# Block-diagonal state of a retention kernel: four full-width products in place of eight half-width column-tiled ones

## The chip, the cores and the metric

The kernel runs on one core of one Trainium2 chip. The time is device time in microseconds (us), the median of several executions. Executions of one kernel mostly agree within 0.3%, so a change of 1% is visible and one of 0.2% is not. TensorE (PE) is the matmul engine; its weight loads are listed separately as PEld. DVE, ACT and POOL are the other engines.

Three words are used throughout. A *full-width* product has 128 rows and 128 columns of weights. A *column-tiled* (half-width) product has 128 rows and 64 columns of weights and writes only 64 output partitions; two of them, in different column halves of the array, can run at once. A *row-tiled* product has 64 rows of weights and runs two at a time in the same way. The *columns* of a product are those of its moving operand, which is streamed past the weights. These are three tiling modes of the array.

## The reference, cut to what matters

```python
scores = scale * q @ k^T                      # 8 batches, 8 heads, 576 positions, 64 per head
ret    = scores * where(i >= j, gamma_h ** (i - j), 0)
x      = heads side by side of (ret @ v)      # 4608 x 512
out    = ((x @ w_a) * (x @ w_b)) @ w_out      # 512 -> 1536 -> 512
```

## The kernel before

The sequence is cut into 36 chunks of 128 tokens, nine for every two batches. Within a chunk, masked scores times v give one part of the output. The earlier chunks enter through a running state, k^T v, a 64x64 block for each head. Two heads share one 128x128 tile of the state, which is therefore block-diagonal (the blocks off the diagonal are zeros). Both parts are accumulated in the same tile `o` of PSUM, the memory for matmul results:

```python
    def outputs(i, halves=False):
        ...
        o = ps_att.tile([128, HP, 128], FP32, tag="att", name="o")   # HP = 4 head pairs
        if m > 0:                                  # a chunk with a state before it
            st = state_of.pop(i)
            n = 64 if m == MID else 128            # the middle chunk of nine spans two batches
            for p in range(HP):
                for hi in (0, 1):                  # state product, column-tiled
                    nc.tensor.matmul(o[64 * hi:64 * hi + 64, p, 0:n],
                                     st[:, p, 64 * hi:64 * hi + 64],
                                     qkT[:, 0, p, 0:n],
                                     start=(p == 0), stop=True,
                                     skip_group_check=True)
        for p in range(HP):
            for hi in (0, 1):                      # masked product, column-tiled
                e0 = p * 128 + 64 * hi
                nc.tensor.matmul(o[64 * hi:64 * hi + 64, p, :],
                                 vb[:, e0:e0 + 64], sT[:, hi, p, :],
                                 start=(m == 0 and p == 0), stop=True,
                                 skip_group_check=True)
```

The rest of TensorE's work is the feed-forward part: full-width products, most of 512 moving columns. The attention of later chunks is put into that stream in three stages, mostly for two adjacent chunks at a time:

```python
    def second_stage(g):
        for i in g[1:]:
            state(i)              # k^T v ("kv"), full-width (64 rows in the middle chunk)
        for i in g:
            scores(i)             # row-tiled

    def third_stage(g):
        flush()
        for i in g:
            outputs(i)            # the code above, for both chunks in one run
```

Of the kernel before, what the change touches and what calls it, by code (L numbers as in the profile page):

```python
# [18 lines left out]
def kernel(  # L19
# [19 lines left out]
    nc = tc.nc  # L39
# [17 lines left out]
    def rows_of(i):  # L57

        b, m = 2 * (i // PER), i % PER
        if m < MID:  # L60
            return [(0, 128, b, 128 * m)]
        if m == MID:
            return [(0, 64, b, 128 * m), (64, 64, b + 1, 0)]
        return [(0, 128, b + 1, 64 + 128 * (m - MID - 1))]
# [201 lines left out]
    def outputs(i, halves=False):  # L266
        m = i % PER
        qkb, qb, kb, vb = natural.pop(i)
        qkT = transposed.pop(i)
        sT = scored.pop(i)  # L270
        o = ps_att.tile([128, HP, 128], FP32, tag="att", name="o")
        if m > 0:
            st = state_of.pop(i)
            n = 64 if m == MID else 128
            for p in range(HP):
                for hi in (0, 1):
                    nc.tensor.matmul(o[64 * hi:64 * hi + 64, p, 0:n],  # L277
                                     st[:, p, 64 * hi:64 * hi + 64],
                                     qkT[:, 0, p, 0:n],
                                     start=(p == 0), stop=True,  # L280
                                     skip_group_check=True)
        for p in range(HP):
            for hi in (0, 1):
                e0 = p * 128 + 64 * hi
# [4 lines that stand above are left out]
        s0 = rows_of(i)[0][3]  # L289

        def scaled(c0, c1):
            nc.vector.tensor_tensor(  # L292
                xT[:, c0:c1, i * 128:(i + 1) * 128], o[:, c0:c1],
                qs[:, c0:c1, s0:s0 + 128], op=ALU.mult)

        if halves:
            later.append(lambda: scaled(0, HP // 2))
            later.append(lambda: scaled(HP // 2, HP))
        else:
            later.append(lambda: scaled(0, HP))  # L300
# [83 lines left out]
    for i in range(4):  # L384
        if idle[i][0]:
            warm(idle[i][0])
        scores(i)
        flush()
        if i == 2:
            load_w(0, W1)  # L390
            load_w(W1, W2)
        if i < 3:
            cast(i + 1, "dve" if i == 2 else "act")
        state(i)
        if idle[i][1]:
            warm(idle[i][1])
        if i < 3:
            transposes(i + 1)
            outputs(i)
            flush()  # L400
    load_w(W2, DFF)
    for i in (0, 1, 2):
        load_wo(i)
    outputs(3, halves=True)
    flush()
    nc.sync.dma_start(gate, wo_sb[0:1, 3, 0:64])
# [39 lines left out]
# [3 lines that stand above are left out]
            outputs(i)  # L449
# [73 lines left out]
```

## Time and profile before

| | before |
|---|---|
| median of 3 executions | 346.77 us (345.89 to 347.11) |
| span of the profiled execution | 877.8 us |
| TensorE busy | 97% of the span |
| feed-forward products, in units of 512 columns | 1296 |
| half-width state products / masked products | 256 / 288 |

These are lines of the profile page of that execution: the span, the busy time of each engine (with its share of the span and the number of instructions), and the chain of waits that ended last, by engine.

```profile
span 877.8 us, 6134 instructions
...
PE 854.0 (97%) x2390; PEld 309.4 (35%) x2426; DVE 162.0 (18%) x272; ACT 112.6 (13%) x229; POOL 84.3 (10%) x121
...
PE 97%; issue 2%; DMA 1%; SPq 0%; POOL 0%; DVE 0%; ACT 0%
```

TensorE holds 97% of that chain, so what changes its stream should change the time. But the span is two and a half times the timed one, and this page has no row for TensorE's granted clock. Its durations can't be taken as costs. The spacing between matmuls can still be read, because it falls into a few sharp values: most 512-column products start 621 ns apart, others 485, and 128-column ones 56 or about 189 ns. Each is 53 to 56 ns per 128 columns plus a whole number of stalls of about 136 ns.

The timeline of TensorE around the outputs of one pair of chunks shows what the change is about. Columns: start in us, length in us, engine, line of the kernel, operation, output <- inputs, weights as rows*columns, moving operand, number.

```profile
start us, us, engine line op out<-in xcount [idle before <-releaser]
305.81 0.79 PE L349 MATMUL po<-wo_sb,hT 128*128 128x512 bf16 x1
306.52 0.69 PE L277 MATMUL o<-qkT,state_166 128*64 128x128 bf16 x8
306.90 0.93 PE L285 MATMUL o<-sT,vb 128*64 128x128 bf16 x8
307.52 0.80 PE L277 MATMUL o<-qkT,state_167 128*64 128x128 bf16 x8
308.14 0.80 PE L285 MATMUL o<-sT,vb 128*64 128x128 bf16 x8
309.26 0.92 PE L349 MATMUL po<-wo_sb,hT 128*128 128x512 bf16 x1 [0.32 <-issue]
```

Eight half-width state products (L277) or masked products (L285) take 0.62 us from the start of one group to the start of the next (307.52 to 308.14), which is the same as one 512-column product takes in this execution. So the eight ran as four pairs of 128 columns. (The first group, 306.52 to 306.90, took only 0.38 us; it was stalled less.) And the first state product starts 0.71 us after the 512-column product before it, not 0.62: there is a gap of about 0.09 us at the change of tiling mode.

### The profile page before, as it was taken

The page shows a single profiled execution, that of the slowest core. Times are in us where ns is not written, and L with a number is a line of the kernel's source. Part 1 is how long each engine was busy: PE and PEld are TensorE (multiplying, and loading weights), DVE is VectorE, ACT ScalarE, POOL GpSimd, SP SyncE. Part 2 cuts the span into 40 slices and gives each one's busy share as a digit, 9 for nine tenths or more (in the row PEclk, how much of TensorE's full clock was granted, in tenths as well). Part 3 has the DMA queues.
Part 4 walks back from the last instruction along what each step waited for, and adds up shares of the span by engine and source line. Part 5 has one row for each costly group of instructions (what it writes and reads, how often), then busy time and mean ns, then how long its engine had stood idle before and what let it go on. Part 6 is the DMA issues. An engine that isn't in the chain of part 4 may idle for free.

```text
span 877.8 us, 6134 instructions
## 1 busy us (share of the span) xinstructions
PE 854.0 (97%) x2390; PEld 309.4 (35%) x2426; DVE 162.0 (18%) x272; ACT 112.6 (13%) x229; POOL 84.3 (10%) x121
## 2 busy tenths in 40 slices
PE   6999999999999999999999999999999999999998
PEld 3322345344344333333333333432333333232223
DVE  4211122222121111211122112121121112201100
ACT  5111112011011101100111011101110011101110
POOL 6040002201011010002100210011000000000000
DMA  9980049350090041025400650066002300000000
GB/s 181 207 152 0 25 90 187 80 88 1 29 199 0 13 102 18 0 50 108 81 1 1 131 108 1 0 112 129 0 1 60 61 0 1 8 28 12 0 13 36
DMA packets 154333, 50.74 MB, mean 58 GB/s; under 512 B 144960, under 2 KB 149824, under 8 KB 154304
## 3 DMA queue, kind: packets, MB, share of 16 engines
q1 hardware_dynamic: 149552, 45.63, 26.6%
q0 software_dynamic: 4752, 4.72, 3.4%
q8 instruction: 19, 0.31, 0.2%
q14 instruction: 10, 0.08, 0.0%
HBM read 37.75 MB, written 9.44 MB: 54 GB/s over the span
## 4 chain that ended last, share of the span: by engine, by line
PE 97%; issue 2%; DMA 1%; SPq 0%; POOL 0%; DVE 0%; ACT 0%
PE pb L329 29%; PE pa L316 29%; PE po L349 28%; PE o L285 2%; PE kv L235 2%; PE o L277 2%; PE w L372 1%; PE tp L218 1%; DMA kf<-in_k_dram 1%; SPq L104 0%; POOL qkb L195 0%; PE sc_2460 L252 0%; PE sc_2449 L252 0%; PE sc_1402 L252 0%; PE sc_3677 L252 0%
## 5 line engine op out<-in xcount | busy, mean ns | idle before, releaser
L329 PE MATMUL pb<-xT,wb_sb 128*128 128x512 bf16 (+2 forms) x471 | 279.9, 775 | 2.7 <-issue 2.7
L316 PE MATMUL pa<-xT,wa_sb 128*128 128x512 bf16 (+2 forms) x472 | 277.3, 769 | 3.6 <-issue 3.1
L349 PE MATMUL po<-wo_sb,hT 128*128 128x512 bf16 (+1 forms) x425 | 253.2, 810 | 6.2 <-issue 6.2
L334 DVE TENSOR_TENSOR hT<-ha,pb 128x512 bf16<-128x512 bf16 (+2 forms) x120 | 76.2, 635 | 457.4 <-PE pb L329 443.3
L329 PEld LDWEIGHTS <-wb_sb 128*128 128x128 bf16 x480 | 82.8, 172 | 173.7 <-issue 168.0
L316 PEld LDWEIGHTS <-wa_sb 128*128 128x128 bf16 x480 | 80.7, 172 | 157.2 <-issue 151.4
L349 PEld LDWEIGHTS <-hT 128*128 128x128 bf16 x444 | 73.1, 169 | 162.1 <-issue 159.0
L322 ACT CAST ha<-pa 128x512 bf16<-128x512 f32 (+2 forms) x120 | 65.2, 544 | 447.1 <-PE pa L316 440.9
L196 POOL TENSOR_TENSOR vb<-vf,vs 128x512 bf16<-128x512 f32 x36 | 37.6, 1044 | 295.1 <-issue 144.3
L189 POOL CAST qkb<-qf 128x512 bf16<-128x512 f32 x30 | 18.3, 611 | 290.5 <-DMA qf<-in_q_dram 274.6
L360 DVE COPY osb<-po 128x512 f32<-128x512 f32 (+1 forms) x17 | 11.5, 676 | 175.5 <-PE po L349 175.5
L358 ACT COPY osb<-po 128x512 f32<-128x512 f32 (+1 forms) x20 | 11.5, 576 | 219.3 <-PE po L349 208.4
L292 DVE TENSOR_TENSOR xT<-o,qs 128x512 bf16<-128x512 f32 (+1 forms) x37 | 24.8, 674 | 46.8 <-PE o L285 46.8
L285 PE MATMUL o<-sT,vb 128*64 128x128 bf16 x288 | 30.4, 379 | 0.0
L235 PE MATMUL kv<-vb,qkb 128*128 128x128 bf16 (+1 forms) x128 | 25.4, 373 | 1.4 <-issue 0.9
L235 PEld LDWEIGHTS <-qkb 128*128 128x128 bf16 (+1 forms) x128 | 17.6, 161 | 22.2 <-issue 20.9
L285 PEld LDWEIGHTS <-vb 128*64 128x64 bf16 x288 | 22.3, 181 | 2.5 <-issue 2.5
L195 POOL CAST qkb<-kf 128x512 bf16<-128x512 f32 x32 | 19.7, 616 | 13.6 <-DMA kf<-in_k_dram 13.5
L252 PEld LDWEIGHTS <-qkT 64*128 64x128 bf16 x288 | 15.4, 135 | 12.6 <-issue 9.8
L218 PE MATMUL tp<-identity,qkb 128*128 128x128 bf16 x48 | 8.1, 362 | 6.0 <-ACT qkb L191 5.3
L372 PE MATMUL w<-identity 128*128 128x512 bf16 x14 | 9.3, 790 | 0.0
L218 PEld LDWEIGHTS <-qkb 128*128 128x128 bf16 x48 | 5.2, 140 | 11.1 <-ACT qkb L191 5.7
(195 smaller groups left out, 194.7 us busy)
## 6 DMA issues: line engine op xcount, KB each, us to landing
out_dram<-osb SPq DMA_DIRECT2D x35, 256.0 KB, 2.2
qf<-in_q_dram SPq DMA_DIRECT2D x32, 256.0 KB, 3.6
kf<-in_k_dram SPq DMA_DIRECT2D x32, 256.0 KB, 4.2
vf<-in_v_dram SPq DMA_DIRECT2D x32, 256.0 KB, 4.7
wo_sb<-in_moe_w_out_dram POOLq DMA_DIRECT2D x3, 512.0 KB, 17.8
qf<-in_q_dram SPq DMA_DIRECT2D x8, 128.0 KB, 3.6
kf<-in_k_dram SPq DMA_DIRECT2D x8, 128.0 KB, 3.5
vf<-in_v_dram SPq DMA_DIRECT2D x8, 128.0 KB, 3.5
```

The lines of the kernel that those rows point to most:

```text
L189: nc.gpsimd.tensor_copy(qb, qf)
L195: nc.gpsimd.tensor_copy(kb, kf)
L196: nc.gpsimd.tensor_tensor(vb.rearrange("p (h d) -> p h d", h=H), vf.rearrange("p (h d) -> p h d", h=H), vs[:, i % PER, :].unsqueeze(2).to_ ...
L218: nc.tensor.transpose(tp[:, p, :], natural_qk[w][:, p * 128:(p + 1) * 128], identity)
L235: nc.tensor.matmul(kv[:, p, :], kb[r, sl], vb[r, sl], start=(m in (0, MID) and p == 0), stop=True, skip_group_check=True)
L285: nc.tensor.matmul(o[64 * hi:64 * hi + 64, p, :], vb[:, e0:e0 + 64], sT[:, hi, p, :], start=(m == 0 and p == 0), stop=True, skip_group_che ...
L292: nc.vector.tensor_tensor(xT[:, c0:c1, i * 128:(i + 1) * 128], o[:, c0:c1], qs[:, c0:c1, s0:s0 + 128], op=ALU.mult)
L316: nc.tensor.matmul(pa[:, 0:n], wa_sb[:, c, fs], xT[:, c, tok0:tok0 + n], start=(c == 0), stop=(c == NC - 1))
L322: nc.scalar.copy(ha[:, 0:n], pa[:, 0:n])
L329: nc.tensor.matmul(pb[:, 0:n], wb_sb[:, c, fs], xT[:, c, tok0:tok0 + n], start=(c == 0), stop=(c == NC - 1))
L334: nc.vector.tensor_tensor(hT[:, F, 0:n], has[F][:, 0:n], pb[:, 0:n], op=ALU.mult)
L349: nc.tensor.matmul(po[:, 0:width], hT[:, F, u * 128:(u + 1) * 128], wo_sb[:, F, cols], start=(F == 0), stop=(F == NF - 1))
```

## The change

The intent: as the state is block-diagonal with explicit zeros, one full-width product gives both heads of a pair at once, so eight loads and eight matmuls become four and four. The result is the same.

```diff
             for p in range(HP):
-                for hi in (0, 1):
-                    nc.tensor.matmul(o[64 * hi:64 * hi + 64, p, 0:n],
-                                     st[:, p, 64 * hi:64 * hi + 64],
-                                     qkT[:, 0, p, 0:n],
-                                     start=(p == 0), stop=True,
-                                     skip_group_check=True)
+                nc.tensor.matmul(o[:, p, 0:n], st[:, p, :],
+                                 qkT[:, 0, p, 0:n],
+                                 start=(p == 0), stop=True,
+                                 skip_group_check=True)
```

## The prediction

> **What bounds it now.** TensorE. The page gives PE busy 97% of the span, and the chain of waits that ended last is 97% PE; DVE is busy 18%, ACT 13%. What the change does to TensorE's stream lands on the time almost in full.
>
> **A caution.** The profiled execution took 877.8 us, the timed ones 346.77 us. In the timeline 512-column matmuls start mostly 621 ns apart, 384-column ones 432, 256-column ones 245, 128-column ones 56 or about 189: 53 to 56 ns per 128 columns, plus stalls of about 136 ns. I take the stalls for something of the profiled execution: 1296 full-size feed-forward products at 4 x 53.5 ns are 277 us, which with a prologue of some 28 us, attention of some 34 us and a tail just fills 346.77 us. So I cost with unstalled spacings.
>
> **Removed.** For each of 32 chunks with a state, eight half-width products (128x64 weights, 128 columns) become four of 128x128: 128 weight loads and 128 matmuls fewer.
>
> **What that saves: about nothing.** The half-width products already ran two at a time: their pairs start 53 to 56 ns apart where nothing stalls, and eight take 621 ns, like one 512-column matmul. Four full-width products of 128 columns (the kv products) also start 56 ns apart unstalled, and four take 621 ns. Weight loads hide in both cases: half-width loads (110 ns each, overlapped) kept the 56 ns spacing, as do kv's full-width ones (98 ns). The Trainium skill, "TensorEngine Tiling (Array Packing)", Restrictions, says that column tiling disables Fast Weight Load; in this trace that costs nothing visible.
>
> **What it adds: tiling switches.** The same page, Key Properties, says that changing the tiling mode drains TensorE. The trace agrees: a state product after a 512-column matmul starts 715 ns after it, where full-width followers start after 621; scores (row-tiled) after 718; leaving scores costs 282 instead of 189. So a switch costs about 94 ns. Before, state and masked-score products of two adjacent chunks are one column-tiled run: one switch in, one out. After, the full-width state sits between column-tiled runs. For a single chunk the count stays; for a pair whose second chunk has a state, two are added. Counted in the instruction order of both programs: 87 before, 113 after, 26 more (13 pairs). 26 x 94 ns = 2.4 us, all critical. The other engines' order is unchanged.
>
> **Prediction.** 346.77 + 2.4, less a few tenths for fewer instructions in the prologue: **349.0 us**, range 346.6 to 351.0. Faster by over 2%: 0.02; within 2%: 0.94; slower by over 2%: 0.04.
>
> **What the profile would show.**
> - State matmuls: 128 instead of 256, full-width, 56 or 189 ns apart; four take about as long as the eight did.
> - The first state product after a 512-column matmul starts 621 instead of 715 ns after it.
> - The first half-width product after a state starts about 94 ns late, and so does a state after half-width products in a pair.
> - Unchanged: DVE, ACT, DMA, feed-forward spacings. The profiled span moves by less than 1%, unless the stalls depend on instruction count, which I don't expect.
>
> **What would make it wrong.** If the timed execution, without stalls, exposes weight loads that the stalls hide (half-width loads then cost more, and the change gains up to some 4 us); if instruction issue limits the attention bursts there (also a gain); or if a drain between short products costs less, or more, than the 94 ns seen after long ones.

## The result, and the profile after

| | before | after |
|---|---|---|
| median | 346.33 us (345.86 to 347.11, 4 executions) | 349.10 us (348.60 to 349.86, 4 executions) |
| ratio after / before | | 1.008, 95% interval 1.0059 to 1.0101 |

Every ratio in this document is the mean time of one kernel's executions over that of the other's in the same rounds, so it is not quite the ratio of the medians. Executions over 1.5% slower than the fastest of the same kernel are left out of the means. 0.8% of 346.5 us is 2.8 us.

The profile after is a clean one. The same parts of its page, and the row of the granted clock (tenths of full speed in 40 slices):

```profile
span 347.5 us, 5914 instructions
...
PE 334.3 (96%) x2298; PEld 174.1 (50%) x2298; DVE 162.3 (47%) x272; ACT 112.3 (32%) x229; POOL 85.2 (25%) x121
...
PEclk9999999999999999999999999999999999999999
...
PE 91%; DMA 4%; DVE 1%; SPq 1%; POOL 0%; issue 0%; ACT 0%; DVEq 0%
```

For a fair comparison of traces the kernel before was profiled again; this is run e0_before of the experiments below. These are lines of that page:

```profile
span 344.4 us, 6170 instructions
...
PE 331.2 (96%) x2426; PEld 172.1 (50%) x2426; DVE 160.7 (47%) x272; ACT 112.4 (33%) x229; POOL 85.0 (25%) x121
...
PEclk9999999999999999999999999999999999999999
...
PE 86%; DMA 8%; SPq 2%; POOL 1%; issue 1%; DVE 1%; ACT 0%; POOLq 0%
```

This one isn't stalled: 344.4 us, full clock. TensorE holds 86% of its chain. The long DMA pieces of the chain lie in the first 9 us, between 65 and 93 us and in the last 6 us; time added to TensorE in the middle stretch can vanish in a wait. After the change TensorE has 128 matmuls fewer (2298 instead of 2426), and the span is longer. Now the line of the state products in the list of costliest groups, first of the second profile of before, then of after (busy time in us, mean ns of one, idle time before them):

```profile
L277 PE MATMUL o<-qkT,state 128*64 128x128 bf16 (+1 forms) x256 | 12.8, 222 | 0.0
```

```profile
L276 PE MATMUL o<-qkT,state 128*128 128x128 bf16 (+1 forms) x128 | 12.3, 220 | 0.0
```

Half the number of products, and the busy time is nearly the same, 12.8 and 12.3 us. Busy time counts an interval in which two products overlap once. So this line shows that the half-width products ran in pairs; it shows neither a gain nor the loss. The loss is in the timeline. First TensorE around the outputs of one pair of chunks in the second profile of the kernel before:

```profile
129.38 0.38 PE L349 MATMUL po<-wo_sb,hT 128*128 128x512 bf16 x1
129.69 0.41 PE L277 MATMUL o<-qkT,state 128*64 128x128 bf16 x8
129.94 0.39 PE L285 MATMUL o<-sT,vb 128*64 128x128 bf16 x8
130.16 0.39 PE L277 MATMUL o<-qkT,state 128*64 128x128 bf16 x8
130.38 0.39 PE L285 MATMUL o<-sT,vb 128*64 128x128 bf16 x8
130.71 0.39 PE L349 MATMUL po<-wo_sb,hT 128*128 128x512 bf16 x1
```

Then the same pair in the profile after:

```profile
130.24 0.59 PE L347 MATMUL po<-wo_sb,hT 128*128 128x512 bf16 x2
130.67 0.39 PE L276 MATMUL o<-qkT,state 128*128 128x128 bf16 x4
130.99 0.41 PE L283 MATMUL o<-sT,vb 128*64 128x128 bf16 x8
131.34 0.40 PE L276 MATMUL o<-qkT,state 128*128 128x128 bf16 x4
131.66 0.41 PE L283 MATMUL o<-sT,vb 128*64 128x128 bf16 x8
132.01 0.39 PE L347 MATMUL po<-wo_sb,hT 128*128 128x512 bf16 x1
```

Before, the four groups follow each other 0.22 to 0.25 us apart. After, they are 0.32 to 0.35 us apart, although each has the same four stretches of 128 columns. From the start of the last 512-column product before the run to the start of the first one behind it: before, 129.38 to 130.71, which is 1.33 us; after, 1.56 us (the line x2 at 130.24 is two products 0.215 us apart, so the last one starts at 130.457, and the next one starts at 132.01).

The start-to-start times of neighbouring matmuls, computed from the two traces, name every step (ns, the usual value):

| from -> to | before | after |
|---|---|---|
| 512-column product -> state product | 309 | 216 (no change of mode) |
| state -> masked product | 53 | 149 |
| masked product -> state of the second chunk | 53 | 152 |
| masked product -> 512-column product | 152 | 152 |
| full-width products of 128 columns within a group (state, kv) | 56 | 56 |
| pairs of half-width products within a group | 56 | 56 |
| first to second pair behind a change to column tiling | 80 | 80 |
| kv (full) -> scores (row-tiled) | 152 | 152 |
| scores -> 512-column product | 149 | 149 |

A change of mode costs 93 to 99 ns beyond the usual distance of the same products: 93 into column tiling, 96 into and out of row tiling, and 99 out of column tiling (152 instead of 53). A column-tiled group that follows a change pays another 24 ns before its second pair, and a full-width group that follows a column-tiled one pays 10 ns (66 instead of 56 between its first two). For a pair of chunks this makes 93 + 99 + 24 + 10 = 226 ns, against 1553 - 1326 = 227 ns measured.

To check the total, I summed over the 18 places in which a run of output products stands in the feed-forward stream. At each place I took the time from the last feed-forward product to the next, less that product's own columns. The sum is 17.69 us before and 20.38 us after: +2.69 us. In the first pair, which waited about 0.4 us for masked scores before, that wait shrank to 0.2 us and took up the whole addition; the other twelve pairs paid in full. The profiled span after is longer by 3.1 us (347.5 - 344.4). Beside the 2.69 us, the prologue before the first feed-forward product took 1.8 us more (23.3 and 21.5 us), and the places with scores 1.4 us less (15.50 and 16.86 us), because the scores of some early chunks waited less: TensorE reached two of these places 1.8 and 1.2 us later, and they took 0.6 and 0.8 us less. That these two terms are not of the change's making is likely but not shown by the profiles alone. With full-width states the prologue took 21.5, 21.5, 22.0, 23.3 and 23.5 us in five profiles, so the width doesn't force the longer one; but in the four with all or most of the states half-width it was 21.5 to 21.8 us. In the two long ones TensorE once waited 1.7 and 1.9 us for a copy on DVE (L193). The timed executions of e1 below, all full-width, show no loss from it.

### The profile page after: what moved, and what is told of

Its sections match the earlier page's. It is cut to its first block, busy times and chain, and to the rows that moved or that the text cites. A ratio compares the mean times of both kernels' runs of the same rounds, so it can differ in the third digit from the quotient of the medians.

```text
span 347.5 us, 5914 instructions
## 1 busy us (share of the span) xinstructions
PE 334.3 (96%) x2298; PEld 174.1 (50%) x2298; DVE 162.3 (47%) x272; ACT 112.3 (32%) x229; POOL 85.2 (25%) x121
## 4 chain that ended last, share of the span: by engine, by line
PE 91%; DMA 4%; DVE 1%; SPq 1%; POOL 0%; issue 0%; ACT 0%; DVEq 0%
PE pa L314 27%; PE pb L327 27%; PE po L347 25%; PE o L283 4%; PE sc L252 3%; PE o L276 2%; PE kv L235 2%; DMA kf<-in_k_dram 1%; DMA qkT<-qkb 1%; PE w L370 1%; SPq L104 1%; PE tp L218 1%; DMA qf<-in_q_dram 1%; DMA out_dram<-osb 1%; DVE qkb L193 1%; DVE sT L258 0%
## 5 line engine op out<-in xcount | busy, mean ns | idle before, releaser
L314 PE MATMUL pa<-xT,wa_sb 128*128 128x512 bf16 (+2 forms) x480 | 111.7, 358 | 0.5 <-DVE xT L290 0.5
L327 PE MATMUL pb<-xT,wb_sb 128*128 128x512 bf16 (+2 forms) x480 | 111.5, 358 | 0.0
L347 PE MATMUL po<-wo_sb,hT 128*128 128x512 bf16 (+1 forms) x444 | 98.2, 374 | 0.0
L327 PEld LDWEIGHTS <-wb_sb 128*128 128x128 bf16 x480 | 46.9, 98 | 46.5
L314 PEld LDWEIGHTS <-wa_sb 128*128 128x128 bf16 x480 | 45.1, 98 | 43.8 <-issue 0.5
L347 PEld LDWEIGHTS <-hT 128*128 128x128 bf16 x444 | 41.6, 98 | 45.9
L258 DVE TENSOR_TENSOR sT<-sc,mask 128x512 bf16<-128x512 f32 x72 | 47.3, 684 | 4.9 <-PE sc L252 4.2
L283 PE MATMUL o<-sT,vb 128*64 128x128 bf16 x288 | 15.5, 229 | 0.0
L252 PE MATMUL sc<-qkT 64*128 64x128 bf16 x288 | 12.9, 223 | 1.5 <-DVE xT L290 0.7
L235 PE MATMUL kv<-vb,qkb 128*128 128x128 bf16 (+1 forms) x128 | 12.8, 224 | 0.2 <-POOL vb L196 0.2
L276 PE MATMUL o<-qkT,state 128*128 128x128 bf16 (+1 forms) x128 | 12.3, 220 | 0.0
```

The source lines that it names most:

```text
L235: nc.tensor.matmul(kv[:, p, :], kb[r, sl], vb[r, sl], start=(m in (0, MID) and p == 0), stop=True, skip_group_check=True)
L252: nc.tensor.matmul(ps[hi][:, p, :], qkT[r, 1, p, :], qkT[r, 0, p, :], start=True, stop=True, skip_group_check=True)
L258: nc.vector.tensor_tensor(sT[:, hi], ps[hi], keep.unsqueeze(1).to_broadcast([128, HP, 128]), op=ALU.mult)
L283: nc.tensor.matmul(o[64 * hi:64 * hi + 64, p, :], vb[:, e0:e0 + 64], sT[:, hi, p, :], start=(m == 0 and p == 0), stop=True, skip_group_che ...
L314: nc.tensor.matmul(pa[:, 0:n], wa_sb[:, c, fs], xT[:, c, tok0:tok0 + n], start=(c == 0), stop=(c == NC - 1))
L327: nc.tensor.matmul(pb[:, 0:n], wb_sb[:, c, fs], xT[:, c, tok0:tok0 + n], start=(c == 0), stop=(c == NC - 1))
```

## The experiments

**Theory.** The loss is 26 more changes of tiling mode (counted in the instruction order: 87 before, 113 after), on TensorE's critical stream. These counts take all kv products as full-width. Those of the middle chunks have 64 rows, and the traces show a change around them too (312 ns behind a 512-column product, 148 ns to the next one); with them it is 91 and 117. The difference stays 26. **Rival.** Full-width products or loads with 128 moving columns are themselves dearer than pairs of half-width ones ("width theory"). A third possibility, tested on the side, is a bad place in the schedule that has nothing to do with the number of changes. All runs gave correct results.

### e0_before: the kernel before, unchanged

No edit: a control, and the unstalled profile used above.

> The kernel before, unchanged, run once more: a control, and a profile of it without the stalls that spoilt the first one. All theories: ratio 1.000 within 0.2%. Switch theory: without stalls, a column-tiled product after a 512-column matmul starts about 311 ns after it (216 + 95), leaving costs about 150 instead of 56, and there is nothing between state and masked-score products; a pair of chunks, from the start of the last matmul before it to the start of the first after it, takes about 1330 ns, where the changed kernel's trace has 1554.

Measured: 346.13 us, ratio 0.9994 (0.9979 to 1.0009). The profile showed what was expected: 309 ns in, 152 out, 53 between state and masked products, and 1326 ns for the pair. The stalls of the first profile were thus not a property of this kernel's executions.

### e1_states_first: full width, but the old number of mode changes

```diff
-        for i in g:
-            outputs(i)
+        os = [(i, outputs_state(i)) for i in g]      # full-width state products of both chunks
+        for i, o in os:
+            outputs_masked(i, o)                     # then the masked products of both
```

(`outputs` is cut into two functions at the blank between its two loops; the products are those of the changed kernel.)

> All state products full-width as in the change, but for a pair of chunks both states' products come first and then both chunks' masked-score products: 87 changes of tiling mode, as before the change, instead of 113. Switch theory: the loss is gone, ratio to before 1.000 (0.998 to 1.002), 346.4 us. Width theory (full-width loads or products themselves cost more than half-width pairs): the loss stays, ratio 1.008.

Measured: 346.34 us, ratio 1.000 (0.9987 to 1.0013). The loss is gone. This is the pair of the timelines above in e1_states_first:

```profile
129.99 0.38 PE L354 MATMUL po<-wo_sb,hT 128*128 128x512 bf16 x1
130.21 0.61 PE L277 MATMUL o<-qkT,state 128*128 128x128 bf16 x8
130.75 0.64 PE L290 MATMUL o<-sT,vb 128*64 128x128 bf16 x16
131.32 0.60 PE L354 MATMUL po<-wo_sb,hT 128*128 128x512 bf16 x2
```

One change in (130.21 to 130.75: eight products of 56 ns plus 93), one out, and 129.99 to 131.32 is 1.33 us, as in the kernel before. The sum over the 18 places is 17.66 us. Full width costs nothing by itself, and it gains nothing either.

### e2_two_halves: the changed kernel's products, with 64 more mode changes

```diff
-            for p in range(HP):
-                ...state product...
-        for p in range(HP):
-            for hi in (0, 1):
-                ...masked product...
+        for half in (range(0, HP // 2), range(HP // 2, HP)):
+            for p in half if m > 0 else ():
+                ...state product...
+            for p in half:
+                for hi in (0, 1):
+                    ...masked product...
```

> The change, with each chunk's work split: states of the first two head pairs, their masked products, states of the last two, their masked products. The same products, 177 changes of mode, 64 more than the change. Switch theory: 64 x 94 to 114 ns on top of 349.1: 355.1 to 356.4 us, ratio to before 1.025 to 1.029. Width theory: as the change, ratio 1.008.

Measured: 355.56 us, ratio 1.0261 (1.0237 to 1.0286). The same products in another order cost 1.8% more than the change. The 18 places sum to 27.01 us, 6.63 us more than after: 104 ns for each of the 64, between the bare 93 to 99 and the 113 (half of the 226 above) that includes the slower starts.

### e3_one_of_four: a quarter of the width, all of the mode changes

```diff
-            for p in range(HP):
+            nc.tensor.matmul(o[:, 0, 0:n], st[:, 0, :],
+                             qkT[:, 0, 0, 0:n], start=True, stop=True,
+                             skip_group_check=True)
+            for p in range(1, HP):
                 for hi in (0, 1):
                     nc.tensor.matmul(o[64 * hi:64 * hi + 64, p, 0:n],
                                      st[:, p, 64 * hi:64 * hi + 64],
                                      qkT[:, 0, p, 0:n],
-                                     start=(p == 0), stop=True,
+                                     start=False, stop=True,
                                      skip_group_check=True)
```

> The kernel before with only the first of the four state products full-width, the other six half-width: a quarter of the change in width, but all of its mode changes (113). Switch theory: the whole loss, ratio 1.008 (1.006 to 1.010), 349.1 us. Width theory: a quarter of it, ratio 1.002.

Measured: 349.71 us, ratio 1.0091 (1.0076 to 1.0107): the whole loss with a quarter of the width, so the width theory falls. In the timeline of this kernel one full-width product (L275) sits in front of each chunk's half-width ones, state (L280) and masked (L288):

```profile
130.83 0.22 PE L275 MATMUL o<-qkT,state 128*128 128x128 bf16 x1
130.98 0.36 PE L280 MATMUL o<-qkT,state 128*64 128x128 bf16 x6
131.17 0.39 PE L288 MATMUL o<-sT,vb 128*64 128x128 bf16 x8
131.49 0.23 PE L275 MATMUL o<-qkT,state 128*128 128x128 bf16 x1
131.65 0.36 PE L280 MATMUL o<-qkT,state 128*64 128x128 bf16 x6
131.84 0.39 PE L288 MATMUL o<-sT,vb 128*64 128x128 bf16 x8
```

The one product of 128 columns takes 0.15 us and 0.16 us until the next group starts, where 0.056 would do; state to masked, 130.98 to 131.17, has no such gap, and is three pairs long. The 18 places sum to 20.40 us; after the change it was 20.38.

### e4_longer_runs and e5_longer_half: fewer mode changes than before

If the number of changes is what counts, longer runs should gain. From chunk 12 on, the outputs of four chunks are put in one run (scores still by pairs), with 75 changes of mode, 12 fewer than before. (With the 64-row kv products counted, it is 77 against 91, so 14 fewer: one more group of these products lies next to scores, which are row-tiled as well.) e4 has full-width states as in e1, e5 the half-width ones of the kernel before.

```diff
+    plan = [(((11,),), starts[11] - 16)] + [
+        (((i, i + 1), (i + 2, i + 3)), starts[i] - 28)
+        for i in range(12, NCH, 4)]
+    for halves, third in plan:
+        for j, g in enumerate(halves):
+            second = third - 36 - 38 * (len(halves) - 1 - j)   # scores, by pairs
+            ...
+        todo.append((third, third_stage, (sum(halves, ()),)))    # outputs of all four
     ...
-    states = [... for i in range(4)]
+    states = [... for i in range(6)]
     def second_stage(g):
+        flush()
```

> Full-width states, states first, and from chunk 12 on the outputs of four chunks in one run instead of two (scores still by pairs): 75 changes of mode instead of 87. Switch theory: six runs fewer, each saving a way in (94 ns and about 24 ns of start) and a way out (95 ns) as the second profile of the kernel before shows: 6 x 213 ns = 1.3 us, ratio to before 0.996 (0.994 to 0.999), if the earlier scores and the larger burst bring no new wait. A theory that the loss came from anything but the number of changes (a bad place in the schedule, say) expects 1.000.

> The same runs of four chunks with the half-width state products of the kernel before: 75 changes of mode. Switch theory: the same 0.996, within 0.2% of the full-width version, since the width of the state products costs nothing by itself. Width theory: below the full-width version by 0.5% or more.

Measured: 349.96 us, ratio 1.0104 (1.0073 to 1.0136), and 349.92 us, ratio 1.0084 (1.0065 to 1.0104). The expected gain did not appear. The runs of outputs did get shorter: in e4 they sum to 16.36 us (12 places now), 1.33 us less than before, as expected. But the places with scores sum to 20.38 us, against 16.86 before. The first lines of the view of who waited for whom, in e4 (engine and line waiting, for whom, us in total, times, longest):

```profile
engine line waited for: us in total, times, longest us
PE tp L218 <- ACT qkb L191: 5.3, 1, 5.3
PE sc L252 <- DVE sT L258: 4.5, 5, 1.1
```

The scores (L252) waited five times, together 4.5 us, for DVE's masking of earlier scores (L258). My own schedule did this: the second score run of four chunks stood right behind the last masking of the first, whose buffer it needs. As for width, the two kernels are equal within 0.2%, which is what the switch theory expects. (The medians differ by 0.04 us; the ratio of e4 is raised by one execution of 353.14 us, the others are at most 350.83.)

### e6_longer_spaced and e7_spaced_half: the same with the score runs farther apart

```diff
-            second = third - 36 - 38 * (len(halves) - 1 - j)
+            second = third - 36 - 48 * (len(halves) - 1 - j)
```

> As e4_longer_runs, with the two score runs of four chunks 48 instead of 38 work units apart. In e4 the second score run stood right behind the last masking of the first and waited for its buffer some 1.0 to 1.2 us in five places; with 16 units between, those waits should be gone from the chain of waits. Then the switch theory expects what it did of e4: 75 changes of mode, 1.3 us less than before, ratio 0.996 (0.993 to 0.999). If the ratio stays at 1.008 or more, the waits weren't what e4 lost by.

> The same spacing with half-width state products. Switch theory: 0.996, within 0.2% of e6_longer_spaced.

Measured: 344.35 us, ratio 0.9931 (0.9914 to 0.9948), and 344.14 us, ratio 0.9930 (0.9914 to 0.9945). Both beat the kernel before and the changed one, and the width of the state products makes no difference. The same view in e6:

```profile
engine line waited for: us in total, times, longest us
PE tp L218 <- ACT qkb L191: 5.7, 2, 5.3
PE sc L252 <- DMA qkT<-qkb: 2.4, 3, 1.4
PE po L354 <- issue: 1.4, 9, 0.2
```

The scores no longer wait for DVE's masking, here or in the rest of that view. The line "po <- issue" is no wait: this trace holds 2265 of the program's 2298 matmuls, and a missing record of a 512-column product leaves a seeming gap of 0.16 us behind a 128-column one. Eight of the 12 runs of outputs end in such a hole, each 226 ns longer than the same run in e4, and a ninth has a kv group next to it (0.22 us); without these they sum to 16.36 us, as in e4, and 1.3 us less than before. The places with scores, one of them with such a hole as well, take 16.69 us (before: 16.86). So of the 1.6 us by which the profiled spans differ (344.4 and 342.8) the longer runs make 1.3. The gain in the timed executions, 2.4 us, is larger; the spans of the kernel before vary there from 344.1 to 346.0 us, those of e6 from 342.2 to 342.9, and where the other 0.8 us come from is not settled. The new schedule also moves the scores and loads of later chunks, and the experiments did not separate that. A bad place in the schedule, the third possibility, expected no gain from longer runs; the 1.3 us by which the runs of outputs shrank, in e4 as in e6, speak against it.

## Why the prediction was right, point by point

The forecast was 349.0 us, which is 346.77 + 2.4 less a few tenths; measured were 349.10 us and +2.8 us. That the two times agree within 0.1 us is partly luck: the base turned out 0.4 us lower (346.33), and the rise 0.5 us higher than the 2.2 us from 346.77 to 349.0.

- *TensorE bounds the kernel, so its stream is the time.* Right, though less fully than the 97% of the stalled profile says: without stalls it is 86% of the chain, and one of the 13 pairs lost its addition in a wait. The 2.69 us that the 18 places gained agree with the +2.8 us of the timed executions.
- *The stalls belong to the profiled execution.* Right: the second profile of the same kernel has none, and 512-column products are 216 ns apart in it. The rough budget that supported this was right only in its sum: in that profile the prologue takes 21.5 us, not 28, and the attention in the stream, its waits included, 38.9 us, not 34. Had the 877.8 us been taken at face value, a product of 128 columns would have seemed to cost up to 189 ns instead of 56.
- *The halving saves about nothing.* Right. Half-width pairs and full-width products both run 56 ns apart unstalled, and loads hide in both cases. e1 (1.000) shows it in time, e6 against e7 shows it again.
- *26 changes of mode at 94 ns, 2.4 us.* Right in the number and nearly in the size. The bare cost is 93 to 99 ns. What the sum left out are the slower starts behind a change, 24 and 10 ns, which make it some 113 ns for each change added, less one pair that hid its addition in a wait it had anyway.
- *A few tenths less for fewer instructions in the prologue.* Not shown. The prologue was 21.5 us in the unstalled profile before and 23.3 us after, and varied by 2 us among the profiles with full-width states.
- *The profiled span moves by less than 1%.* Against the stalled 877.8 us this can't be judged; against the second profile it is 0.9% (347.5 and 344.4 us).
- *What would make it wrong: exposed loads, issue limits, another drain cost.* None occurred. The spacings of the unstalled profile are those that were picked out of the stalled one.

On the pages: the Trainium skill, "TensorEngine Tiling (Array Packing)", section Key Properties, says that changing the tiling mode drains TensorE; these traces agree in that each change costs 93 to 99 ns. Its section Restrictions says that column tiling disables Fast Weight Load, which is by its name a quicker way to load weights. The loads of 64 columns are indeed not shorter than those of 128 (medians 110 and 98 ns), but this cost no time, because they overlap with the matmuls. The records also tell when the load behind a change begins. Within a mode, a load mostly starts 54 ns before its product (behind a 128-column one) or 214 ns (behind a 512-column one). Behind a change it starts only 1 to 5 ns before, in the traces before and after alike, although a load lasts 93 to 106 ns there (medians). So the lost time lies before the load and not in it: load and product are both held back. That it is the drain that holds them these runs don't show.

## What to carry to other kernels

Before merging half-width products into full-width ones, look at whether the half-width ones already run two at a time: then halving their number saves nothing. Count the changes of tiling mode in TensorE's order of instructions: each costs here some 93 to 113 ns, as much as two products of 128 columns, so put products of one mode next to each other, as e1 does by doing the states of both chunks first, and e6 by longer runs. Busy time doesn't show this cost; the start-to-start times at the seams do.

## What the Trainium skill lacked or had wrong

- "TensorEngine Tiling (Array Packing)", Key Properties: the drain is named without a size. These runs show 93 to 99 ns for each change of mode, nearly the same in both directions and for row and for column tiling, and 93 or 94 ns into column tiling behind products of 512, 128 or 64 columns (a 64-column state product is followed after 123 ns instead of 29).
- The same page doesn't tell of a slower start behind a change: 80 instead of 56 ns to the second half-width pair, 66 instead of 56 ns between the first two full-width products.
- "TensorE: Matmul & The Clock Gate", Back-to-back issue gap, gives a sustained roofline for streams of one load per matmul of about 81 ns at 128 columns and about 131 ns at 512. In these traces it is 56 ns and 216 ns, with a new load for each matmul; the isolated-gap formula of the same section (128/2.4 + 2.5 and 512/2.4 + 2.5 ns) fits both.
- No page tells of a profiled execution like the first one here: 877.8 us for a program of 347 us, no clock records, and stalls of about 136 ns in the stream of matmuls. A second profile of the same kernel was free of them.
